# Wider selection, sum and maximum-spread products in the first 24 heads of a batched decode attention block

## The chip, the cores and the metric

The kernel runs on one core of one Trainium2 chip. The metric is the device time of one execution in microseconds (us); lower is better. The engines are named as in the profile: PE is TensorE's matmul stream, PEld its weight loads, DVE is VectorE, ACT is ScalarE, POOL is GpSimd and SP is SyncE, which issues nearly all DMAs here.

## The reference, cut to what matters

An adaLN-conditioned decode step for four batch rows, one token each. It has cached attention (32 query heads that share 8 key/value heads, 4,096 cached positions, head size 128, all in float32), then a token-mixing MLP.

```python
mod = (silu(c) @ w_mod).reshape(4, 6, 1, 512)
h = layernorm(x) * (1 + ca) + sa
q = (h @ wq) ...                              # 32 heads of 128
scores = einsum("bhqd,bhkd->bhqk", q, k) * 128 ** -0.5
o = einsum("bhqk,bhkd->bhqd", softmax(scores), v)
x = x + ga * (o.reshape(4, 1, 4096) @ wo)
h = layernorm(x) * (1 + cb) + sb
u = gelu(einsum("bsd,sf->bdf", layernorm(h), w1) + b1)
x = x + gb * (einsum("bdf,fs->bds", u, w2) + b2).transpose
```

The key and value caches are 4 x 8 x 4096 x 128 floats each, 134 MB in all, and every one of them is read once.

## The kernel before

The work goes head by head, over 32 pairs of a batch row and a key/value head ("head i" below, i from 0 to 31; REP = 4 query heads share each). Keys and values come in tiles of 4 MB that hold the key of head i+2 and the value of head i; a ring of three such tiles is shared with the weights that are loaded first (`load_pair`, L174, issued on SP). A tile is free for the next load when the last product that reads it is done, so SP's queue waits for that.

For one head the steps are these, with the line of the main instruction:

- `scores` (L231): eight products of 512 columns, four 32-row quadrants of the result side by side; `row_max` (L236, DVE) takes the maximum of each row.
- `turn_max` (L240, a transpose on PE), `col_max` (L245, DVE), `spread_max` (L251, a product with the constant -1 that puts the negated maximum on all partitions), `copy_max` (L256, DVE), and `expo` (L261, ACT, the exponential and its row sums).
- `turn` (L267/L271, DVE, transposes the probabilities in 32 x 32 blocks), `sums` (L275, one product that adds the row sums up over the blocks and spreads them) and `scale` (L280, DVE, reciprocal).
- `values` (L291): eight products of 512 columns; `copy_v` (L314, DVE) takes the result out of PSUM.
- `pick` (L328): four products with a 128-column stationary block of the copied result and a selection of four columns as the moving operand; they select and add up the pieces and leave a 128 x 4 result. `copy_o` (L335, DVE) multiplies it by the reciprocals, and `project` (L343) and `add_up` (L359, L361, DVE) multiply by the rows of wo and add up.

Every float32 product shows as two weight loads and two matmuls in the trace. So one pick is eight records, one `sums` or `spread_max` is two.

The first 24 heads run in a Python loop that is a little software pipeline: iteration i does scores of head i+2, pick of i-1, transposes and sums of i+1, values of i. From head 8 on the loop also carries the MLP of the batch row that is done (`Mixer`; `expand` L442 on DVE, gelu L506 on ACT, `consume` L453 on PE). The loop ends with values of head 23; the rest of the work, among it pick of head 23 and everything of heads 24 to 31 that is left, stands in a hand-written order, `PLAN` (L667), and after it the last row's MLP (`finish`). Engines take their instructions in the order of the program.

`pick` can already stream its selection several times: `WIDE` (L24) gives the number of copies of the four columns, 24 for head 27 and 32 for head 28. All copies but the first are left unread (`OT[i] = pt[:, 0]`).

Of the kernel before, what the change touches and what calls it, by code (L numbers as in the profile page):

```python
# [8 lines left out]
F32 = mybir.dt.float32  # L9
# [5 lines left out]
B, D, HQ, HKV, SK, DH, F = 4, 512, 32, 8, 4096, 128, 1792  # L15
REP = HQ // HKV
NF = F // 128
EPS = 1e-5
P = 128
NS = B * HKV  # L20
NSM = 3 * NF + 16 + 1


WIDE = {NS - 5: 24, NS - 4: 32}  # L24
NARROW = NS - 3


# [1 line left out]
def adaln_decode(ctx: ExitStack, tc: tile.TileContext, small, x, wmod, wq, kk, kv, vv, wo, out):  # L29
    nc = tc.nc  # L30
    pad = ctx.enter_context(tc.tile_pool(name="pad", bufs=1))
# [7 lines left out]
    ps_m = ctx.enter_context(tc.tile_pool(name="ps_m", bufs=2, space=PSUM))  # L39
    ps_e = ctx.enter_context(tc.tile_pool(name="ps_e", bufs=1, space=PSUM))  # L40
    ctx.enter_context(tc.manual_schedule())
    mm = nc.tensor.matmul
    dv = nc.vector

    neg1 = pad.tile([1, 96], F32, name="neg1")[:, 0:1]
    sm = cst.tile([P, NSM], F32, name="sm")
    xr = wk.tile([P, D], F32, name="xr", tag="yw", bufs=1)[0:B]
    wm01 = ring.tile([P, 2, 4, D], F32, name="wm01", tag="kv")
# [17 lines left out]
    nc.gpsimd.tensor_scalar(w1n, w1, -1.0, None, op0=OP.mult)  # L66
    ones = cst.tile([P, P], F32, name="ones")
    nc.gpsimd.memset(ones, 1.0)
    nc.gpsimd.memset(neg1, -1.0)
    part = cst.tile([P, 1], F32, name="part")  # L70
    nc.gpsimd.memset(part, -1.0 / D)
    half = cst.tile([P, 1], F32, name="half")
# [11 lines left out]
    eight = g32.rearrange("p (r x) -> p r x", x=8)[:, :, 0]  # L84
# [42 lines left out]
    for k in range(4):  # L127
        n = slice(k * P, (k + 1) * P)
# [95 lines left out]
    S, M, PL, RL = {}, {}, {}, {}  # L224
# [22 lines left out]
        M[i] = mx  # L247

    def spread_max(i):
        pb = ps_m.tile([P, 1], F32, name="pb", tag="m")  # L250
        mm(pb, M[i].rearrange("o c r -> o (c r)"), neg1, start=True, stop=True)  # L251
        M[i] = pb

    def copy_max(i):
        nm = wk.tile([P, 1], F32, name="nm")
# [15 lines left out]
            dv.transpose(p, p)  # L271

    def sums(i):
        pl = ps_m.tile([P, REP], F32, name="pl", tag="m")
        mm(pl, PL[i][1].to_broadcast([P, P]), eight, start=True, stop=True)  # L275
        RL[i] = pl

    def scale(i):
        rl = wk.tile([P, REP], F32, name="rl", bufs=4)
# [38 lines left out]
    def pick(i):  # L318
        po = PV.pop(i)
        n, m = po.shape[-1] // DH, WIDE.get(i, 1)  # L320
        if i in OT:
# [290 lines left out]
    for i in range(2):  # L612
        for step in (scores, row_max, turn_max, col_max, spread_max, copy_max, expo):
            step(i)
    for step in (turn, sums, scale):
        step(0)
    mix = None
    for i in range(NS - HKV):
# [7 lines left out]
        if i:  # L626
            pick(i - 1)
            copy_o(i - 1)
        turn(i + 1)
        sums(i + 1)  # L630
        scale(i + 1)
        if i:
# [3 lines left out]
        col_max(i + 2)  # L636
        values(i, range(4))
        spread_max(i + 2)
        copy_max(i + 2)
        expo(i + 2)  # L640
# [16 lines left out]
        if i == NS - HKV - 2:  # L657
# [17 lines left out]
    g T2 zs za zx zq c c zm zb0 T3 zv zb1 zw0 zn zc  # L675
    """
    TABLE = {"s": scores, "S": row_max, "m": turn_max, "X": col_max, "b": spread_max, "B": copy_max, "e": expo,
             "l": sums, "L": scale, "V": copy_v, "a": pick, "A": copy_o, "P": add_up,
             "LP": load_pair}
    MIX = {"F": mix.fold, "R": mix.residual, "G": mix.gather, "M": mix.modulate, "H": mix.gather, "Q": mix.spread,  # L680
# [3 lines left out]
    for step in PLAN.split():  # L684
        op, k = step.rstrip("0123456789."), step.lstrip("abcdefghijklmnopqrstuvwxyzABCDEFGHIJKLMNOPQRSTUVWXYZ")
        i, q = (int(n) for n in (k + ".0").split(".")[:2]) if k else (0, 0)
# [102 lines left out]
```

## Time and profile before

| | |
|---|---|
| median of three runs | 386.45 us (386.39 to 386.74) |
| span of the profiled execution, first to last instruction | 384.7 us |
| median less span (start and end outside the instructions) | 1.75 us |
| mean granted TensorE clock | 0.883 of full speed |
| PE busy / DVE busy / ACT busy | 78% / 52% / 29% of the span |
| moved by DMA | 157.69 MB, mean 410 GB/s |

Times in the trace count from the first instruction. The page names no time of the profiled execution other than its span, so sums are made against the 384.7 us and carried over to the median with the 1.75 us.

### The profile page before, as it was taken

To read this page: it belongs to the slowest core of one execution; us is meant where nothing else is said; L and a number is where in the kernel's file an instruction comes from. 1 tells how busy PE (TensorE), PEld (TensorE's weight loads), DVE (VectorE), ACT (ScalarE), POOL (GpSimd) and SP (SyncE) were. 2 spreads that over 40 slices of the span, in tenths; PEclk is the share of its full clock that TensorE was granted. 3 is DMA by queue.
4 is the path that set the end of the run, shared out by engine and by line. 5 is a ranking of instruction groups with operands and counts; after the bars stand their busy time and mean duration, and the time that the engine had idled before them with its cause. 6 is when DMAs were issued, how large, how long until landed. Compare 5 with 4: busy or idle time off the path is not lost.

```text
span 384.7 us, 5604 instructions
## 1 busy us (share of the span) xinstructions
PE 298.7 (78%) x2380; PEld 117.2 (30%) x2380; DVE 198.2 (52%) x407; ACT 112.2 (29%) x144; POOL 7.7 (2%) x33
## 2 busy tenths in 40 slices
PE   0856777866966949979877878788888887999984
PEld 0112122311323313334322222342222343333653
DVE  1130251620451424664866545557665567778757
ACT  1001111121110110212567311124575105657276
POOL 1100000000000000000000000000000000000000
PEclk9989555985695685998999998999999999999999
DMA  8999999999999999999999999999999999999930
GB/s 331 433 433 436 411 453 433 409 432 436 423 441 433 434 436 436 434 436 431 429 425 433 428 433 434 429 433 431 429 434 436 434 436 432 424 417 423 418 122 3
DMA packets 7409, 157.69 MB, mean 410 GB/s; under 512 B 964, under 2 KB 1236, under 8 KB 1496
## 3 DMA queue, kind: packets, MB, share of 16 engines
q1 hardware_dynamic: 7376, 157.33, 95.4%
q8 instruction: 18, 0.29, 0.3%
q14 instruction: 7, 0.06, 0.0%
q10 hardware_dynamic: 8, 0.00, 0.0%
HBM read 157.32 MB, written 0.01 MB: 409 GB/s over the span
## 4 chain that ended last, share of the span: by engine, by line
DMA 60%; PE 29%; DVE 7%; ACT 2%; issue 1%; POOL 0%; SPq 0%; POOLq 0%; DVEq 0%
DMA kv<-in_kv 58%; PE s L231 8%; PE pv L291 7%; PE s L122 2%; PE qs L138 2%; DVE m L236 2%; DVE p L267 2%; DMA sm<-in_small 2%; PE pa L343 2%; PE pt L328 2%; ACT uu L562 1%; PE pb L251 1%; PE pve L303 1%; PE pm L240 1%; PE pgx L348 1%
## 5 line engine op out<-in xcount | busy, mean ns | idle before, releaser
L231 PE MATMUL s<-kv,QT 128*32 128x512 f32 x512 | 75.2, 714 | 38.9 <-DMA kv<-in_kv 37.0
L236 DVE TENSOR_REDUCE m<-s 128x1 f32<-128x1024 f32 x32 | 39.2, 1224 | 96.0 <-PE s L231 95.9
L261 ACT ACTIVATE p<-s,nm 128x1024 f32<-128x1024 f32 x32 | 35.7, 1115 | 180.6 <-DVE nm L256 180.5
L291 PE MATMUL pv<-kv,p 128*32 128x512 f32 x464 | 69.8, 670 | 0.7 <-DMA kv<-in_kv 0.7
L231 PEld LDWEIGHTS s<-kv,QT 128*32 128x32 f32 x512 | 15.8, 123 | 84.0 <-DMA kv<-in_kv 52.5
L328 PEld LDWEIGHTS pt<-g,po 128*128 128x128 f32 x236 | 31.1, 205 | 27.2 <-issue 19.9
L343 PE MATMUL pa<-wo,oT 128*32 128x512 f32 x240 | 34.6, 648 | 4.6 <-DVE oT L335 4.4
L328 PE MATMUL pt<-g,po 128*128 128x4 f32 (+2 forms) x236 | 33.9, 267 | 1.5 <-DVE po L314 1.0
L267 DVE STREAM_TRANSPOSE p<-p 128x1024 f32<-128x1024 f32 x25 | 30.9, 1234 | 0.0
L314 DVE COPY po<-pv 128x512 f32<-128x512 f32 x29 | 20.0, 688 | 16.8 <-PE pv L291 16.7
L245 DVE TENSOR_REDUCE mx<-pm 1x128 f32<-1x512 f32 x32 | 21.3, 669 | 1.1 <-PE pm L240 1.1
L442 DVE TENSOR_SCALAR u<-hb,wr,sm 128x512 f32<-128x512 f32 x40 | 19.9, 541 | 1.9 <-POOL wr L437 1.0
L506 ACT ACTIVATE u<-u 128x1024 f32<-128x1024 f32 x20 | 20.4, 1051 | 1.5 <-DVE u L442 1.4
L361 DVE TENSOR_TENSOR acc<-acc,pa 128x512 f32<-128x512 f32 x26 | 17.8, 686 | 4.3 <-PE pa L343 4.2
L261 ACT ACT_TABLE_LOAD x11 | 14.1, 1283 | 20.3 <-DVE nm L256 20.2
L251 PEld LDWEIGHTS pb<-neg,mx 1*128 1x128 f32 x64 | 10.4, 202 | 28.2 <-DVE mx L245 26.5
L122 PE MATMUL s<-wm,sT 128*4 128x512 f32 x16 | 9.1, 732 | 10.6 <-DVE sT L108 10.6
L506 ACT ACT_TABLE_LOAD x13 | 16.7, 1283 | 0.2
L291 PEld LDWEIGHTS pv<-kv,p 128*32 128x32 f32 x464 | 13.4, 146 | 7.2 <-issue 3.1
L240 PE MATMUL pm<-ident,m 128*1 128x128 f32 x32 | 9.3, 289 | 7.4 <-DVE m L236 3.5
L251 PE MATMUL pb<-neg,mx 1*128 1x1 f32 x64 | 13.1, 271 | 2.1 <-DVE mx L245 2.1
L453 PE MATMUL py<-u,sm 128*32 128x512 f32 x80 | 14.4, 616 | 0.0
(158 smaller groups left out, 214.7 us busy)
## 6 DMA issues: line engine op xcount, KB each, us to landing
kv<-in_kv SPq DMA_DIRECT2D x28, 4096.0 KB, 21.9
wq<-in_wq SPq DMA_DIRECT2D x2, 4096.0 KB, 16.3
wo<-in_wo SPq DMA_DIRECT2D x4, 2048.0 KB
kv<-in_kv SPq DMA_DIRECT2D x4, 2048.0 KB, 20.3
wm<-in_wmod SPq DMA_DIRECT2D x2, 2048.0 KB, 14.8
kv<-in_kk SPq DMA_DIRECT2D x1, 4096.0 KB
kv<-in_vv SPq DMA_DIRECT2D x3, 1024.0 KB
wm<-in_wmod SPq DMA_DIRECT2D x1, 1024.0 KB
```

The costliest lines, as they stand in the source:

```text
L231: mm(s[32 * c:32 * c + 32, n * 512:(n + 1) * 512], QT[:, b, h, :], KT[i][:, (n * 4 + c) * 512:(n * 4 + c + 1) * 512], start=True, stop=True)
L236: dv.tensor_reduce(M[i], S[i], axis=AX.X, op=OP.max)
L245: dv.tensor_reduce(mx, M[i].rearrange("o (c r) -> o r c", c=4).unsqueeze(1).to_broadcast([1, 4, 32, 4]), axis=AX.X, op=OP.max)
L251: mm(pb, M[i].rearrange("o c r -> o (c r)"), neg1, start=True, stop=True)
L261: nc.scalar.activation(p, S[i], AF.Exp, bias=M.pop(i), accum_out=l)
L267: dv.transpose(PL[i][0], PL[i][0])
L291: mm(PV[i][32 * q:32 * q + 32, :], pT[:, 128 * k:128 * k + 128:4], VT[i][:, 4 * k:4 * k + 4, :].rearrange("p j d -> p (j d)"), start=(k < ...
L314: dv.tensor_copy(PV[i], pv)
L328: mm(pt, po[:, c * DH:(c + 1) * DH], sel.unsqueeze(1).to_broadcast([P, m, REP]), start=(c == 0), stop=(c == n - 1))
L343: mm(pa[32 * g:32 * g + 32, :], oT[:, g:g + 1].to_broadcast([P, 32]), wo_t[h][:, g, :], start=True, stop=True)
L442: dv.tensor_scalar(u[:, e, :], hb, wr[:, j:j + 1], b1[:, j:j + 1], op0=OP.mult, op1=OP.add)
L506: nc.scalar.activation(u, u, AF.Gelu_apprx_tanh)
```

## The change

In heads 0 to 23 three small products stream more columns than are read. `pick` streams its selection of four columns 64 times over (256 columns in place of 4), `sums` streams its four columns 64 times (256 in place of 4), and `spread_max` multiplies by 96 constants in place of one. The readers take the first copy. The tile `neg1` was already 96 wide; its memset on POOL now fills all of it. Number and order of instructions, tiles and buffers stay the same, as do heads 24 to 31.

```diff
-WIDE = {NS - 5: 24, NS - 4: 32}
+WIDE = {NS - 5: 24, NS - 4: 32, **{i: 64 for i in range(NS - HKV)}}
...
-    neg1 = pad.tile([1, 96], F32, name="neg1")[:, 0:1]
+    negs = pad.tile([1, 96], F32, name="neg1")
+    neg1 = negs[:, 0:1]
...
-    nc.gpsimd.memset(neg1, -1.0)
+    nc.gpsimd.memset(negs, -1.0)
...
     def spread_max(i):
-        pb = ps_m.tile([P, 1], F32, name="pb", tag="m")
-        mm(pb, M[i].rearrange("o c r -> o (c r)"), neg1, start=True, stop=True)
-        M[i] = pb
+        n = 96 if i < NS - HKV else 1
+        pb = ps_m.tile([P, n], F32, name="pb", tag="m")
+        mm(pb, M[i].rearrange("o c r -> o (c r)"), negs[:, 0:n], start=True, stop=True)
+        M[i] = pb[:, 0:1]
...
     def sums(i):
-        pl = ps_m.tile([P, REP], F32, name="pl", tag="m")
-        mm(pl, PL[i][1].to_broadcast([P, P]), eight, start=True, stop=True)
-        RL[i] = pl
+        m = 64 if i < NS - HKV else 1
+        pl = ps_m.tile([P, m, REP], F32, name="pl", tag="m")
+        mm(pl, PL[i][1].to_broadcast([P, P]), eight.unsqueeze(1).to_broadcast([P, m, REP]), start=True, stop=True)
+        RL[i] = pl[:, 0]
```

## Rows read from the trace of the kernel before

**Rows 1.** The page: span, PE's busy time, and two lines by 40 slices.
```profile
span 384.7 us, 5604 instructions
PE 298.7 (78%) x2380; PEld 117.2 (30%) x2380; DVE 198.2 (52%) x407; ACT 112.2 (29%) x144; POOL 7.7 (2%) x33
...
PEclk9989555985695685998999998999999999999999
DMA  8999999999999999999999999999999999999930
```
**Rows 2.** The page, DMA issues: KB each, median us from issue to landing.
```profile
kv<-in_kv SPq DMA_DIRECT2D x28, 4096.0 KB, 21.9
```
**Rows 3.** Windows: length, busy us per engine, PEclk, DMA share, GB/s.
```profile
61.50:317.00 255.50, 203.65 (x1463) 76.85 (x1464) 132.41 (x252) 66.70 (x84) 3.20 (x7) 0.88 1.00 432
317.00:369.50 52.50, 48.37 (x567) 24.66 (x569) 39.71 (x94) 28.45 (x32) 0.76 (x2) 0.97 0.98 414
```
**Rows 4.** The page: the chain that ended last, by engine.
```profile
DMA 60%; PE 29%; DVE 7%; ACT 2%; issue 1%; POOL 0%; SPq 0%; POOLq 0%; DVEq 0%
```
**Rows 5.** Timeline of PE, one head: start, length, instruction, [idle before <-releaser].
```profile
191.55 1.92 PE L231 MATMUL s<-kv,QT 128*32 128x512 f32 x16 [1.26 <-DMA kv<-in_kv]
...
193.40 1.05 PE L328 MATMUL pt<-g,po 128*128 128x4 f32 x8
...
201.31 1.92 PE L231 MATMUL s<-kv,QT 128*32 128x512 f32 x16 [1.70 <-DMA kv<-in_kv]
```
**Rows 6.** Groups of PE, 184 to 230 us: busy us, mean ns of one.
```profile
L231 PE MATMUL s<-kv,QT 128*32 128x512 f32 x68 | 8.3, 598 | 5.1 <-DMA kv<-in_kv 5.1
...
L328 PE MATMUL pt<-g,po 128*128 128x4 f32 x40 | 5.3, 255 | 0.0
```
**Rows 7.** Timeline of PE: the pick of head 28, already wider.
```profile
356.11 1.16 PE L328 MATMUL pt<-g,po 128*128 128x128 f32 x8
```
**Rows 8.** A stretch at half clock: its window (columns as rows 3) and its pick.
```profile
120.00:128.00 8.00, 8.00 (x39) 2.90 (x31) 3.88 (x6) 0.00 (x0) 0.00 (x0) 0.50 0.97 418
```
```profile
122.43 1.87 PE L328 MATMUL pt<-g,po 128*128 128x4 f32 x8
```
**Rows 9.** The chain in order of time: start, us, what.
```profile
143.25 3.64 PE s L231 x16
...
155.27 16.91 DMA kv<-in_kv
```
**Rows 10.** Timeline of the last loop heads and the plan's first steps.
```profile
289.74 1.92 PE L231 MATMUL s<-kv,QT 128*32 128x512 f32 x16 [1.62 <-DMA kv<-in_kv]
...
293.08 1.06 PE L343 MATMUL pa<-wo,oT 128*32 128x512 f32 x8 [0.21 <-DVE oT L335]
...
300.07 1.92 PE L231 MATMUL s<-kv,QT 128*32 128x512 f32 x16
...
308.09 1.06 PE L328 MATMUL pt<-g,po 128*128 128x4 f32 x8 [0.81 <-DVE po L314]
...
309.35 1.09 PE L291 MATMUL pv<-kv,p 128*32 128x512 f32 x8 [0.20 <-DMA kv<-in_kv]
```
**Rows 11.** Timeline further on in the plan.
```profile
319.02 1.00 DVE L442 TENSOR_SCALAR u<-hb,wr,sm 128x512 f32<-128x512 f32 x2 [1.02 <-POOL wr L437]
...
325.26 1.93 PE L291 MATMUL pv<-kv,p 128*32 128x512 f32 x8
...
343.17 1.92 PE L231 MATMUL s<-kv,QT 128*32 128x512 f32 x16 [0.60 <-DMA kv<-in_kv]
```
**Rows 12.** Windows around the half-clock stretch in the plan (columns as rows 3).
```profile
322.00:325.40 3.40, 1.99 (x18) 0.89 (x14) 3.40 (x7) 0.36 (x1) 0.00 (x0) 1.00 0.96 414
325.40:328.80 3.40, 3.40 (x13) 0.46 (x11) 1.70 (x5) 3.37 (x4) 0.00 (x0) 0.50 0.98 424
```
**Rows 13.** Timeline: the last two waits for cached values.
```profile
362.58 0.81 PEld L303 LDWEIGHTS pve<-kv,p 128*32 128x32 f32 x32 [0.86 <-DMA kv<-in_vv]
...
367.23 0.14 PEld L303 LDWEIGHTS pve<-kv,p 128*32 128x32 f32 x4 [0.17 <-DMA kv<-in_vv]
```

## The prediction

> **What bounds the kernel now.** I read the page's slices first. PE is busy for 78% of the span, which would make it the suspect, but the two lines under it decide: the 16 DMA engines are at 8 or 9 tenths and more in every slice, until they stop in the 39th, at about 368 us [rows 1]. The windows say it more sharply: from 61.5 to 317 us the DMA share is 1.00 at 432 GB/s, and it is 0.98 from there to 369.5 [rows 3]. No time is left over in the stream. The chain that ended last is DMA for 60%, PE for 29% [rows 4]; the PE pieces in the loop lead from a landing to the issue of a later load, as from 143.25 to 155.27 us [rows 9]. So the end is the end of the stream plus the tail behind it (367.4 to 384.7 us), as long as two things hold: no load is issued so late that the stream runs dry, and PE reaches the last landings on time.
>
> How much room does the first have? A load of 4,096 KB lands 21.9 us after its issue [rows 2]; at 432 GB/s it takes 9.7 us itself, so 12.2 us of earlier loads stand ahead of it. That is how late its issue could be. The smallest such case that I saw on the chain is a landing after 16.91 us [rows 9], which leaves 7.2 us.
>
> And the second? In the loop PE waits for keys: 1.26 and 1.70 us ahead of two scores in a row, 9.76 us apart [rows 5]. In the written-out plan it waits 0.60 us at 343.17, and 0.86 and 0.17 us for two of the last pieces of values [rows 11, 13]. The work behind the last of these runs off PE, DVE and ACT and is not touched by the change.
>
> **The change part by part.** It adds no instruction and no DMA and moves none; it makes records longer. The memset of 96 values in place of one is on POOL, ahead of anything that reads it; I cost it at nothing, since POOL is busy for 7.7 us of the whole span with 33 instructions [rows 1], and this one of them can't grow by more than a fraction of that.
>
> A pass of 256 columns is not in the trace. The scores are the nearest by shape: 16 records in 1.92 us, four quadrants side by side, the last record 0.598 us long, so a step of (1.92 - 0.598) / 3 = 0.44 us for 512 columns, 0.22 for 256 [rows 5, 6]. A narrow pick has eight records in 1.05 us, one of them 0.255, so (1.05 - 0.255) / 7 = 0.114 us each [rows 5, 6]: I take the weight loads of 128 columns to set that pace. Going to 0.22 adds 8 x 0.106 = **0.85 us to a pick** and 2 x 0.106 = **0.21 us to `sums`**. The other bound is drawn from a pick that is wide already: 1.16 us for 128 columns [rows 7], 0.11 over the narrow one; by that slope 256 columns come to 1.27, 0.22 over it, and a quarter of that (0.06) for `sums`. Nothing at all is excluded by the 0.11. I take the upper values: 128 columns are where streaming (0.11 by the scores' step) just meets the weight load's 0.114, so the flat slope ends there. `spread_max` with 96 columns stays under the weight load, and two records at the 128-column pick's 0.11 over eight are 0.03 us. So **a head gains 0.3 to 1.1 us of PE work, 1.1 taken**. At half clock (a narrow pick is 1.87 us there, [rows 8]) the columns cost twice that, some 2.1 us.
>
> A rule speaks differently from the row: the Trainium skill, "TensorE: Matmul & The Clock Gate", section "Back-to-back issue gap". It gives N / 2.4 + 2.5 ns for a lone matmul at full clock: 109 ns for 256 columns, less than the 0.114 us that a record of the narrow pick takes now. By that the pick would gain nothing and the lateness worked out below would be gone; the page's figures are for a 16-bit product, and no record here shows 512 columns at that pace.
>
> Where does the 1.1 us go? In heads 0 to 21 it lies beside the stream: PE's waits of 1.26 and 1.70 us per head [rows 5] take it, and if a heavy head did not have them the 7.2 us of queued loads [rows 9] would. Without that cover each head would cost 1.1 us.
>
> The last heads are different, because the plan behind them is dense. Iteration 22 starts on its landing (1.62 us of wait, enough for the 1.1 carried in) [rows 10]. In it the pick and `sums` are wide: 1.06 us, less the 0.21 that PE waits ahead of the projection [rows 10], 0.85. Iteration 23 starts without a wait at 300.07 [rows 10]; its `sums` and `spread_max` belong to heads 24 and 25 and stay narrow, so 0.85 - 0.21 = 0.64. Pick of head 23 stands in the plan at 308.09: 0.85. Together 2.34, less the 0.20 us of wait at 309.35 [rows 10]: the plan starts **2.1 us late** (0.1 by the low bound). What is late next is the first expand on DVE at 319.02, which waited for POOL and no DMA [rows 11], so nothing is taken off there. Then 0.60 us go at 343.17, 0.86 at 362.58, 0.17 at 367.23 [rows 11, 13]: 2.14 - 1.63 = **0.5 us** at the end, 0 by the low bound. Loads stay out of it: those issued in the plan have landings well behind them, as the 12.2 us above say.
>
> One thing works the other way. From 325.4 to 328.8 us the granted clock is 0.50, the lower of the two levels (1.2 and 2.4 GHz), after 3.4 us in which PE was busy for 2.0 at the upper one [rows 12]. Values of head 25 take 1.93 us in it, as against 1.09 for such a step at full clock [rows 10, 11], 0.84 lost; over the whole stretch half its length, 1.7 us, is the most. If the late plan meets it otherwise and the clock stays up, that pays for what is left of the lateness.
>
> So the sum is 384.7 plus 0 to 0.5 of span, and the median 1.75 above: 386.45 to 386.95. I take 386.6.
>
> **Rivals.** A. *The tail takes the lateness up, no change* (forecast), 386.45 to 386.95. This holds whether the clock rises in the loop's half-clock stretches or not: a faster PE there only waits longer for keys. So "the change doesn't do what it says", the clock staying at half in those stretches, is a rival in the mechanism and the same in time, 386.5; half the chance of A is that.
>
> B. *Slower: the plan can't take it.* The waits of 0.60 and 0.86 us belong to PE; if the late chain in the plan is DVE's (row maxima, expands), they give nothing back, and the 2.1 us arrive at the end, perhaps with the half-clock stretch repeated later (1.7 more). For it: DVE is at work for 39.7 of 52.5 us from 317 on and ACT for 28.5 [rows 3]. Against: PE itself is at 48.4 of 52.5 there, and the key that it waits for at 343 us is DMA's. It decides from 0.8 us of unabsorbed lateness on; price 0.8 to 2.1, so 387.3 to 388.6.
>
> C. *Faster: the clock.* 0.88 of full speed in the loop [rows 3] is a loss that wider products might give back, and if the chain were PE's the fall at 325 us alone is 1.7 us: 384.8. Against it stand the landings at 343 and 362 us, which no PE can advance: the gain is held there to what is behind, nothing. Also, PE is busy for all 8 us of a half-clock window at 120 us [rows 8], so being busy was not enough there. The Trainium skill, the same page, section "HAM oscillation — how this bites in real kernels", has the rule behind this rival: gaps in PE's work throttle its clock, and a kernel should keep it fed. The trace agrees in that the fall at 325.4 us follows 3.4 us of which PE stood idle for 1.4 [rows 12].
>
> D. *Slower: the stream runs dry.* If the clock stays at half in the early heads, a head takes the 12.0 us from its key to the next load's issue [rows 9] and 2.1 more, 14.1 against 9.7 of stream; a slack of 7.2 us is gone in the second such head, and each further one costs 4.4 us: 390 and more. Against it: after the first 70 us no two slices in a row stand at 5 [rows 1].
>
> **How the numbers follow.** About 0.2% (0.8 us) is what a measurement of this kernel can tell from no change. A 0.78, B 0.14, C 0.05, D 0.03. The likeliest is A at 386.6, its own range 386.1 to 387.2: the two ends of the sum, with the 0.3 us by which the three runs differ on either side. The range for eight in ten reaches into B's low end: 385.9 to 387.6. Within 0.2%: A, 0.78. Slower: B and D, 0.17. Faster: C, 0.05.
>
> **What the profile afterwards would show.** Right: 432 GB/s and a DMA share of 1.00 in the loop as now; pick records with 256 columns, a group of eight in about 1.9 us at full clock (1.3 would be the low bound); PE's waits ahead of scores in the loop down by about 1 us a head; values of head 24 begun at about 311 us and not 309.35; waits at 343 and 362 us smaller or gone, the last piece of values used at 367 to 368 us. The granted clock is higher in the slices that stand at 5 and 6 now, with no effect on landings. Wrong: a slice in the loop under 420 GB/s with DMA idle; scores of head 30 later than 344.5 us; or a last product of values later than 368.3 us.

## The result and the profile after

The changed kernel takes 387.55 us at the median of nine executions (386.62 to 388.01), the kernel before 386.45 (386.39 to 386.74, nine). The ratio is 1.002, with a 95% interval of 1.001 to 1.0029: slower by about what can be told from no change, and inside the range. What the median hides is a split. Four executions are at 386.62 to 386.85, five at 387.55 to 388.01, and nothing between. The spans (first to last instruction) split a little differently: five lie at 384.7 to 385.1 and four at 385.7 to 386.0. The execution at 387.55, which is the median itself, has a span of only 384.9; its extra 0.8 us or so lies outside the instructions (2.65 us there, against 1.75 to 2.11 in the other eight). Below, the lower and the upper group are those by span. The traced execution is a lower one: 386.62 us, span 384.8. In the experiments 15 of 64 executions of the kernel before stood at 387.8 to 391.3 us, which pulls the ratios there down and widens their intervals; medians and groups are compared beside them.

The page of the changed kernel, the lines that answer to [rows 1, 2, 4]:

```profile
span 384.8 us, 5618 instructions
...
PE 319.2 (83%) x2380; PEld 129.0 (34%) x2380; DVE 200.6 (52%) x407; ACT 112.2 (29%) x144; POOL 8.0 (2%) x33
...
PEclk9989568998796988999999999999999999999999
DMA  8999999999999999999999999999999999999920
...
DMA 43%; PE 41%; DVE 9%; ACT 3%; issue 1%; POOL 1%; SPq 0%; POOLq 0%; DVEq 0%; ACTq 0%
...
kv<-in_kv SPq DMA_DIRECT2D x28, 4096.0 KB, 20.8
```

PE is busy for 20.5 us more. The granted clock is better in seven of the eight slices that stood at 5 and 6. A load lands 20.8 us after its issue at the median, in place of 21.9; with the stream as fast as before that means an issue some 1.1 us later, at the cost of the queued loads alone. PE's share of the chain went from 29% to 41%, and still the span moved by 0.1 us. The windows say why; they answer to [rows 3]:

```profile
61.50:317.00 255.50, 223.85 (x1443) 88.17 (x1447) 132.65 (x246) 66.70 (x84) 2.80 (x6) 0.95 1.00 432
317.00:369.50 52.50, 48.96 (x581) 25.35 (x576) 41.84 (x100) 28.45 (x32) 1.31 (x3) 1.00 0.97 411
```

The loop's clock rose from 0.88 to 0.95 and the stream is at 432 GB/s and a share of 1.00, as before. A better clock bought no landing.

What a wide product costs stands in the groups of PE from 184 to 230 us, beside [rows 6]:

```profile
L331 PE MATMUL pt<-g,po 128*128 128x256 f32 x40 | 10.0, 392 | 0.0
L232 PE MATMUL s<-kv,QT 128*32 128x512 f32 x64 | 7.7, 597 | 0.7 <-DMA kv<-in_kv 0.6
...
L278 PE MATMUL pl<-g,l 128*128 128x256 f32 x10 | 5.1, 600 | 0.0
...
L253 PE MATMUL pb<-neg,mx 1*128 1x96 f32 x10 | 2.3, 308 | 0.9 <-DVE mx L246 0.9
```

The waits for keys ahead of the scores fell from 5.1 to 0.6 us in this stretch: the wider products took most of PE's free time there.

And the last heads of the loop with the plan's start, in the timeline of PE, beside [rows 10, 11, 13]:

```profile
289.56 1.92 PE L232 MATMUL s<-kv,QT 128*32 128x512 f32 x16 [0.24 <-DMA kv<-in_kv]
291.41 2.00 PE L331 MATMUL pt<-g,po 128*128 128x256 f32 x8
293.25 1.02 PE L278 MATMUL pl<-g,l 128*128 128x256 f32 x2
294.21 1.06 PE L346 MATMUL pa<-wo,oT 128*32 128x512 f32 x8
...
301.20 1.92 PE L232 MATMUL s<-kv,QT 128*32 128x512 f32 x16
...
309.99 2.00 PE L331 MATMUL pt<-g,po 128*128 128x256 f32 x8 [0.81 <-DVE po L317]
311.92 1.09 PE L294 MATMUL pv<-kv,p 128*32 128x512 f32 x8
...
321.01 1.09 PE L294 MATMUL pv<-kv,p 128*32 128x512 f32 x8
...
327.47 1.09 PE L294 MATMUL pv<-kv,p 128*32 128x512 f32 x8
...
343.72 1.92 PE L232 MATMUL s<-kv,QT 128*32 128x512 f32 x16
...
365.92 1.92 PE L306 MATMUL pve<-kv,p 128*32 128x128 f32 x60
```

Further lines of the kernel before, for comparison:

```profile
291.59 1.05 PE L328 MATMUL pt<-g,po 128*128 128x4 f32 x8
292.51 0.36 PE L275 MATMUL pl<-g,l 128*128 128x4 f32 x2
...
319.02 1.10 PE L291 MATMUL pv<-kv,p 128*32 128x512 f32 x8 [0.52 <-DMA kv<-in_kv]
...
361.59 1.04 PE L343 MATMUL pa<-wo,oT 128*32 128x512 f32 x8
...
365.61 2.03 PE L303 MATMUL pve<-kv,p 128*32 128x128 f32 x60
```

Values of head 24 begin at 311.92 in place of 309.35: the plan starts 2.57 us late. Scores of head 30 are 0.55 us late at 343.72 and no longer wait for their key, and the last big group of value products is 0.31 us late at 365.92. The tail behind it ends 0.1 us late. Between 311.92 and 343.72 two microseconds came back, at three places. The first half of values of head 25 waited 0.52 us for cached values at 319.02 before; now it begins at 321.01 and waits for none, 1.99 us late and no longer 2.57. The second half takes 1.09 us at 327.47, where it took 1.93 at half clock before [rows 11]: 0.84. And the 0.60 us of wait for the key of head 30 is gone [rows 11].

### The profile page after: what moved, and what is told of

It is laid out like the page before. It is cut to its first block, busy times and chain, and to the rows that moved or that the text cites. A ratio compares the mean times of both kernels' runs of the same rounds, so it can differ in the third digit from the quotient of the medians.

```text
span 384.8 us, 5618 instructions
## 1 busy us (share of the span) xinstructions
PE 319.2 (83%) x2380; PEld 129.0 (34%) x2380; DVE 200.6 (52%) x407; ACT 112.2 (29%) x144; POOL 8.0 (2%) x33
## 4 chain that ended last, share of the span: by engine, by line
DMA 43%; PE 41%; DVE 9%; ACT 3%; issue 1%; POOL 1%; SPq 0%; POOLq 0%; DVEq 0%; ACTq 0%
DMA kv<-in_kv 41%; PE s L232 8%; PE pt L331 8%; PE pv L294 5%; PE pa L346 4%; PE pl L278 3%; PE s L123 2%; PE qs L139 2%; DVE mx L246 2%; DMA sm<-in_small 2%; DVE acc L364 2%; PE pb L253 2%; PE py L456 1%; ACT uu L565 1%; PE pve L306 1%
## 5 line engine op out<-in xcount | busy, mean ns | idle before, releaser
L232 PE MATMUL s<-kv,QT 128*32 128x512 f32 x512 | 72.5, 690 | 23.4 <-DMA kv<-in_kv 21.3
L294 PE MATMUL pv<-kv,p 128*32 128x512 f32 x464 | 63.9, 617 | 0.0
L331 PE MATMUL pt<-g,po 128*128 128x256 f32 (+3 forms) x236 | 56.6, 380 | 1.3 <-DVE po L317 0.8
L331 PEld LDWEIGHTS pt<-g,po 128*128 128x128 f32 x236 | 41.7, 198 | 30.7 <-issue 15.6
L346 PE MATMUL pa<-wo,oT 128*32 128x512 f32 x240 | 31.8, 602 | 0.5 <-DVE oT L338 0.3
L278 PE MATMUL pl<-g,l 128*128 128x256 f32 (+1 forms) x64 | 27.8, 518 | 0.2 <-ACT p L263 0.2
L253 PE MATMUL pb<-neg,mx 1*128 1x96 f32 (+1 forms) x64 | 14.5, 305 | 6.3 <-DVE mx L246 6.1
L338 DVE TENSOR_TENSOR oT<-pt,rl 128x4 f32<-128x4 f32 x30 | 4.8, 161 | 21.0 <-PE pt L331 20.9
## 6 DMA issues: line engine op xcount, KB each, us to landing
kv<-in_kv SPq DMA_DIRECT2D x28, 4096.0 KB, 20.8
```

The costliest lines, as they stand in the source:

```text
L232: mm(s[32 * c:32 * c + 32, n * 512:(n + 1) * 512], QT[:, b, h, :], KT[i][:, (n * 4 + c) * 512:(n * 4 + c + 1) * 512], start=True, stop=True)
L253: mm(pb, M[i].rearrange("o c r -> o (c r)"), negs[:, 0:n], start=True, stop=True)
L278: mm(pl, PL[i][1].to_broadcast([P, P]), eight.unsqueeze(1).to_broadcast([P, m, REP]), start=True, stop=True)
L294: mm(PV[i][32 * q:32 * q + 32, :], pT[:, 128 * k:128 * k + 128:4], VT[i][:, 4 * k:4 * k + 4, :].rearrange("p j d -> p (j d)"), start=(k < ...
L331: mm(pt, po[:, c * DH:(c + 1) * DH], sel.unsqueeze(1).to_broadcast([P, m, REP]), start=(c == 0), stop=(c == n - 1))
L346: mm(pa[32 * g:32 * g + 32, :], oT[:, g:g + 1].to_broadcast([P, 32]), wo_t[h][:, g, :], start=True, stop=True)
```

## The experiments

Theory L (late plan) holds the last heads of the loop responsible, theory E (everywhere) all 24 heads. For the first four kernels the kernel before had a median of 386.51 us on the same chip (35 executions).

**The changed kernel again**, with no edit:

> The changed kernel once more, unedited, as the measure for the other three and for a second trace. Theory L (late plan: the wide products of the last heads of the loop make the written-out plan start 2.6 us late, and an execution ends near 386.8 or near 387.6 depending on whether the clock then falls in the plan): 386.6 to 388.0 again in two groups, and a trace of the upper group shows a half-clock stretch between 320 and 370 us. Theory E (the wide products of all heads cost a little each): all executions near 387.3, one group, and nothing in the plan differs.

Median 386.93 us of twelve executions, 386.46 to 387.74, ratio 0.9985 (0.9958 to 1.0013). Seven lie up to 387.02 and five from 387.27 on, less cleanly parted than the first time. The trace is of a lower one (386.55) and has the clock at full through the plan. Theory E's single group near 387.3 did not come. The trace of an upper execution came later, with the single executions below.

**Wide in heads 0 to 20 only:**

```diff
-WIDE = {NS - 5: 24, NS - 4: 32, **{i: 64 for i in range(NS - HKV)}}
+WIDE = {NS - 5: 24, NS - 4: 32, **{i: 64 for i in range(21)}}
...
-        n = 96 if i < NS - HKV else 1
+        n = 96 if i < 21 else 1
...
-        m = 64 if i < NS - HKV else 1
+        m = 64 if i < 21 else 1
```

> Wide only for heads 0 to 20, so the plan starts on its landing at 309.35 us again. Theory L: 386.45 as before, all executions within 0.3 us of it. Theory E: 21 of 24 parts of what the full change costs, about 387.3. Rival clock theory (more PE work earlier changes the clock in the plan wherever it stands): two groups as in the full change.

Median 386.57 us; eleven of twelve at 386.42 to 386.71, one at 391.26; ratio 0.9988 (0.9955 to 1.002). That is the kernel before. In its trace the windows and the plan's start are:

```profile
61.50:317.00 255.50, 221.31 (x1461) 87.33 (x1462) 134.47 (x252) 66.70 (x84) 3.20 (x7) 0.95 1.00 432
```
```profile
309.50 1.09 PE L294 MATMUL pv<-kv,p 128*32 128x512 f32 x8 [0.45 <-DMA kv<-in_kv]
...
325.44 1.94 PE L294 MATMUL pv<-kv,p 128*32 128x512 f32 x8
...
343.34 1.92 PE L232 MATMUL s<-kv,QT 128*32 128x512 f32 x16 [0.62 <-DMA kv<-in_kv]
```

Nearly all of the extra work and of the clock gain is in it (221.31 us of PE, against 203.65 before and 223.85 in the full change; clock 0.95), and the plan starts on its landing. Theory E falls. The half-clock stretch at 325 us is here, and with the plan on time it costs nothing.

**Wide in heads 21 to 23 only:**

```diff
-WIDE = {NS - 5: 24, NS - 4: 32, **{i: 64 for i in range(NS - HKV)}}
+WIDE = {NS - 5: 24, NS - 4: 32, **{i: 64 for i in range(21, NS - HKV)}}
...
-        n = 96 if i < NS - HKV else 1
+        n = 96 if 21 <= i < NS - HKV else 1
...
-        m = 64 if i < NS - HKV else 1
+        m = 64 if 21 <= i < NS - HKV else 1
```

> Wide only for heads 21, 22 and 23. Theory L: the same as the full change, 386.6 to 388.0 with a median near 387.4, and values of head 24 at about 311.9 us. Theory E: 3 of 24 parts, 386.6 at most, one group.

Median 387.45 us, ratio 0.9991 (0.9964 to 1.0019). Five executions are at 386.76 to 386.91, seven at 387.41 to 387.77: the two groups of the full change from an eighth of its heads. The traced execution is of the upper group, 387.49 us, span 385.7:

```profile
311.97 1.09 PE L294 MATMUL pv<-kv,p 128*32 128x512 f32 x8
...
327.70 1.94 PE L294 MATMUL pv<-kv,p 128*32 128x512 f32 x8
...
344.60 1.92 PE L232 MATMUL s<-kv,QT 128*32 128x512 f32 x16
```

The start is that of the full change; at 327.70 the values run at half clock (1.94 us), and scores of head 30 and the end are 0.9 us later than in the lower group's trace.

**All 24 heads, 128 columns** in pick and sums:

```diff
-WIDE = {NS - 5: 24, NS - 4: 32, **{i: 64 for i in range(NS - HKV)}}
+WIDE = {NS - 5: 24, NS - 4: 32, **{i: 32 for i in range(NS - HKV)}}
...
-        m = 64 if i < NS - HKV else 1
+        m = 32 if i < NS - HKV else 1
```

> All 24 heads wide, but 128 columns in pick and sums in place of 256 (spread of the maximum as in the change). A pick of 128 columns took 1.16 us before against 1.05 for four columns, so 0.1 us a pick and 0.03 a sum: values of head 24 at 309.4 to 309.7 us. Theory L: 386.45 to 386.6, one group. Theory E, if it goes by the count of wide products and not by columns: 387.3; if by time, 386.6 as well.

Median 386.62 us, ratio 0.9983 (0.9956 to 1.001). Ten executions are at 386.41 to 386.80, two at 387.48 and 387.88. These two are not an upper group: their spans are 384.7 and 384.9, as in the other ten (384.5 to 384.7), and the extra time lies outside the instructions. The traced one (386.55) starts the plan at 309.12, not late at all. Its pick and `sums` in iteration 22:

```profile
291.49 1.16 PE L331 MATMUL pt<-g,po 128*128 128x128 f32 x8
292.49 0.60 PE L278 MATMUL pl<-g,l 128*128 128x128 f32 x2
```

The pick costs 0.11 us more than the narrow one. `sums` costs 0.24 more (0.60 in place of 0.36), against 0.03 expected; nearly all of it falls into the 0.21 us that PE waited ahead of the projection before [rows 10]. The number of wide products is that of the full change and the time is that of the kernel before, so it is the time which the products take that counts, not their number.

For the second four kernels the kernel before had a median of 386.53 us (29 executions, another chip).

**Two picks of 512 columns**, heads 22 and 23:

```diff
-WIDE = {NS - 5: 24, NS - 4: 32, **{i: 64 for i in range(NS - HKV)}}
+WIDE = {NS - 5: 24, NS - 4: 32, 22: 128, 23: 128}
...
-        n = 96 if i < NS - HKV else 1
+        n = 1
...
-        m = 64 if i < NS - HKV else 1
+        m = 1
```

> Only the picks of heads 22 and 23 are wide, with 512 columns each; sums and spreads as before. A 256-column pick holds PE for 1.84 us in the changed kernel against 0.92 narrow, so one of 512 columns takes about 3.7, 2.75 more; two of them less the 0.20 us of wait: the plan starts 5.3 us late. Theory L: after the waits of 0.60, 0.86 and 0.17 us, 3.7 us are left at the end, or 2.0 if a half-clock stretch in the plan falls away: 388.4 to 390.2. Rival F (the lateness itself is free and only a fall of the clock in the plan costs, once): 387.6 at most.

Median 389.09 us of ten, ratio 1.0055 (1.0029 to 1.0081). Six are at 388.85 to 389.14, four at 389.59 to 390.03. In the trace (389.04 us, span 387.2) the two picks and the start of the plan:

```profile
302.07 3.71 PE L331 MATMUL pt<-g,po 128*128 128x512 f32 x8
...
310.72 3.71 PE L331 MATMUL pt<-g,po 128*128 128x512 f32 x8 [0.82 <-DVE po L317]
314.36 1.10 PE L294 MATMUL pv<-kv,p 128*32 128x512 f32 x8
...
329.91 1.09 PE L294 MATMUL pv<-kv,p 128*32 128x512 f32 x8
...
346.16 1.93 PE L232 MATMUL s<-kv,QT 128*32 128x512 f32 x16
```

The plan is 5.0 us late at the start, 3.0 at scores of head 30 and 2.5 at the end, with the clock at full (329.91). Rival F, one fixed price, falls: against the lower trace of the full change the plan starts 2.44 us later (314.36 and 311.92) and the span is 2.4 us longer (387.2 and 384.8). What is late beyond the waits of the plan arrives whole.

**Heads 0 to 20 with 512-column picks**, the cover of the loop taken away:

```diff
-WIDE = {NS - 5: 24, NS - 4: 32, **{i: 64 for i in range(NS - HKV)}}
+WIDE = {NS - 5: 24, NS - 4: 32, **{i: 128 for i in range(21)}}
...
-        n = 96 if i < NS - HKV else 1
+        n = 96 if i < 21 else 1
...
-        m = 64 if i < NS - HKV else 1
+        m = 64 if i < 21 else 1
```

> As the kernel with heads 0 to 20 wide, but their picks stream 512 columns: 2.75 us more than narrow, with sums and spread 3.2 a head. Theory L says that the 1.3 us of the change were hidden in heads 0 to 20 because PE waited 1.3 to 1.7 us a head for keys, and 7 to 12 us of loads were queued. With 3.2 that cover is gone from head 8 on, where the MLP runs too: 13 heads late by 1.5 to 1.9 us each, 20 to 25 us in all, of which the queue and the narrow heads behind take about 12: 395 to 400, and a DMA share clearly under 1.00 in the loop. If the loop's work were hidden for another reason (PE not in the way at all), 386.5.

Median 399.1 us of two, ratio 1.0304 (1.0233 to 1.0375). From 200 to 317 us, this kernel first, then the full change:

```profile
200.00:317.00 117.00, 113.03 (x682) 39.93 (x680) 65.67 (x123) 43.38 (x50) 1.31 (x3) 1.00 0.96 393
```
```profile
200.00:317.00 117.00, 107.49 (x731) 43.23 (x727) 70.08 (x133) 42.73 (x50) 1.30 (x3) 1.00 1.01 433
```

PE is busy for 113.03 of the 117 us, the loads come late, and the stream falls to 393 GB/s. So the waits for keys and the queued loads were what hid the change in the loop, and the change used most of the waits.

**Only the pick of head 23:**

```diff
-WIDE = {NS - 5: 24, NS - 4: 32, **{i: 64 for i in range(NS - HKV)}}
+WIDE = {NS - 5: 24, NS - 4: 32, 23: 64}
...
-        n = 96 if i < NS - HKV else 1
+        n = 1
...
-        m = 64 if i < NS - HKV else 1
+        m = 1
```

> Only the pick of head 23 is wide, with 256 columns: the plan starts 0.7 to 0.9 us late. Theory L: the waits of 0.60 and 0.86 us take all of it, 386.45 to 386.6, one group. If a late plan costs whatever its size, 387.2 to 387.5.

Median 386.44 us, all ten at 386.35 to 386.63, ratio 0.9983 (0.9958 to 1.0009). The plan starts at 309.92 in place of 309.35, the second half of values of head 25 meets a half-clock stretch, and scores of head 30 still wait 0.49 us for their key:

```profile
309.92 1.09 PE L294 MATMUL pv<-kv,p 128*32 128x512 f32 x8
...
319.00 1.09 PE L294 MATMUL pv<-kv,p 128*32 128x512 f32 x8
...
325.46 1.43 PE L294 MATMUL pv<-kv,p 128*32 128x512 f32 x8
...
343.07 1.92 PE L232 MATMUL s<-kv,QT 128*32 128x512 f32 x16 [0.49 <-DMA kv<-in_kv]
```

A small lateness is swallowed whole, also with the clock down. What swallowed it is not the waits of 0.60 and 0.86 us that were expected to: at 319.00 PE is already on time again (319.02 before), so the 0.57 us went into the wait of 0.52 for cached values there.

**The full change with wide spreads up to head 27**, an attempt to keep the clock up:

```diff
-        n = 96 if i < NS - HKV else 1
+        n = 96 if i < NS - 4 else 1
```

> The full change, and the spread of the maximum streams 96 columns up to head 27 in place of head 23, so that PE does a little more in the stretch of the plan after which the clock falls in some executions (it waits for DVE from 324.9 to 327.5 us). If the upper group comes from that fall and the fall from PE's little work there: one group, 386.6 to 386.9. If the spreads change nothing of that: two groups as in the full change, 386.5 to 387.8.

Median 387.92 us of twelve (386.65 to 389.39), ratio 1.0006 (0.9973 to 1.0039). Two are below 387, one at 387.15, nine at 387.73 and above. The attempt failed: the upper group did not go, it holds more of the executions. The trace was of the lowest one (386.65, span 384.9), clock at full through the plan.

Last, four single executions with traces, to see both groups of one kernel (386.44 us before).

> The changed kernel, one more trace, to tie the group of an execution to the clock in its plan. Theory L: an execution at 386.5 to 386.9 shows the clock at full from 310 us to the end of the plan and scores of head 30 at 343.6 to 343.9 us; one at 387.3 to 387.8 shows a half-clock stretch between 321 and 345 us, scores of head 30 about 0.9 us later, and no wait for cached values behind. Rival: an upper execution with the clock at full throughout and the extra 0.9 us elsewhere (landings later, or the tail behind 369 us longer).

> As the run before it: the changed kernel, one more trace, same expectations of both theories.

The first is a lower execution (386.80 us, span 385.0), the second an upper one (387.44, span 385.7). The windows of the plan, lower first:

```profile
322.00:326.00 4.00, 3.09 (x29) 0.73 (x21) 4.00 (x9) 1.94 (x2) 0.00 (x0) 1.00 0.96 410
326.00:330.00 4.00, 3.21 (x19) 1.41 (x19) 2.30 (x7) 2.50 (x4) 0.00 (x0) 1.00 1.01 434
330.00:334.00 4.00, 3.54 (x32) 1.15 (x34) 4.00 (x8) 3.97 (x4) 0.00 (x0) 1.00 1.08 467
334.00:369.50 35.50, 34.12 (x452) 18.86 (x450) 28.12 (x71) 18.94 (x23) 0.00 (x0) 1.00 0.95 401
```
```profile
322.00:326.00 4.00, 2.90 (x30) 0.67 (x22) 4.00 (x10) 1.71 (x2) 0.00 (x0) 1.00 0.92 395
326.00:330.00 4.00, 3.47 (x15) 1.21 (x17) 2.30 (x6) 2.73 (x4) 0.00 (x0) 0.68 0.99 426
330.00:334.00 4.00, 4.00 (x34) 1.26 (x34) 2.51 (x6) 3.97 (x4) 0.00 (x0) 0.89 1.12 483
334.00:369.50 35.50, 34.12 (x443) 18.55 (x436) 29.00 (x71) 18.20 (x22) 0.00 (x0) 1.00 0.95 402
```

The same kernel, nearly the same start of the plan (312.13 and 311.91 us), the same 34.12 us of PE work behind 334: what differs is the clock from 326 to 334. Scores of head 30 in the lower one, and three steps of the upper one:

```profile
343.93 1.92 PE L232 MATMUL s<-kv,QT 128*32 128x512 f32 x16
```
```profile
321.00 1.09 PE L294 MATMUL pv<-kv,p 128*32 128x512 f32 x8
...
344.57 1.92 PE L232 MATMUL s<-kv,QT 128*32 128x512 f32 x16
...
366.76 1.92 PE L306 MATMUL pve<-kv,p 128*32 128x128 f32 x60
```

The scores are 0.64 us apart, 0.86 when counted from the start of the plan; that is the price of the half-clock step (1.94 us in place of 1.09). The spans are 0.7 apart, so nothing is added behind 344 us, and neither of the two scores waits for its key. The rival, landings or the tail, is out.

> The kernel with spreads of 96 columns up to head 27, one more trace. Ten of its twelve executions were at 387.1 to 389.4 us, the traced one at 386.7. Theory L: an upper execution shows a half-clock stretch in the plan, as for the changed kernel. Rival: the wider spreads of heads 24 to 27 lengthen the plan's own chain by about 1 us with the clock at full.

387.79 us, span 386.0, an upper execution: half clock again, 0.80 from 326 to 330 and 0.77 from 330 to 334. The wider spreads do not lengthen the plan by themselves: the lower execution of this kernel has a span of 384.9, the full change 384.8 to 385.0.

> The kernel with heads 21 to 23 wide, one more trace. Its traced execution was of the upper group (387.5 us) with a half-clock stretch at 327 us. Theory L: an execution at 386.8 has the clock at full there or the stretch elsewhere, and the same start of the plan at 311.9 to 312.0 us. Rival: the start of the plan differs between the groups.

386.70 us, span 384.9, a lower one: plan from 312.04, clock 1.00 throughout, scores of head 30 at 343.83. So for the full change and for heads 21 to 23 alone each group is traced, and each time the half-clock stretch goes with the upper one.

## Why the prediction was right, and where it was off

**The bound.** Right, and shown: the stream ran at 432 GB/s with either kernel, the work in heads 0 to 20 cost nothing (386.57 us), and it cost 12.6 us when the cover was gone (399.1). Rival C (faster by the clock) is refuted with it: the loop's clock rose to 0.95, and the key that iteration 22 waits for came at 289.56 in place of 289.74, no more than 0.2 us earlier. Rival D did not come; the loop's clock is up, not down.

**The price of a column.** The pick was sized well: the upper bound gave 0.22 us a record, and (2.00 - 0.392) / 7 = 0.23 is what the trace has; a pick holds PE for 1.84 us in place of 0.92 (0.92 more; 0.85 said). A pick of 512 columns takes 3.71 us against 2.00, so it goes nearly by columns there. The Trainium skill's 109 ns ("TensorE: Matmul & The Clock Gate", "Back-to-back issue gap") does not hold for these float32 records; 0.23 us was measured. **`sums` was mis-sized:** 0.21 us said. Two records of 256 columns take 1.02 us, one of them 0.600, so 0.42 a record, nearly twice the pick's. From its start to the projection it held PE for 0.96 us in place of 0.36. It filled the 0.21 us of wait that I had counted as cover, and cost iteration 22 another 0.39 us. A head thus gained 1.5 us from these two products at full clock, more than the 1.1 that I gave as the most for a head.

**The lateness of the plan.** 2.1 us said, 2.57 measured: iteration 22 took 11.64 us from scores to scores in place of 10.33 (1.31 more, 0.85 said), iteration 23 0.77 more to the pick of head 23 (0.64 said), that pick 0.67 beyond the landing (0.65 said). The sum of 2.75 starts 0.18 earlier.

**What is left at the end.** The time is near the sum, but the path to it is not the one that I wrote, and part of the agreement is luck. I took off waits of 0.60, 0.86 and 0.17 us, 1.63 in all; 2.57 - 1.63 = 0.94, and the upper group's span of 385.7 is 1.0 over the 384.7 of before. The traces divide it otherwise. At 319 us I looked at the wait of DVE for POOL and took nothing off; PE waited there as well, 0.52 us for cached values, and in the upper trace the step begins at 321.00, 1.98 us late in place of 2.56. At scores of head 30 it is 1.40 late, so the 0.60 was rightly counted. From there to the last big group of values (366.76) only 0.25 us more goes, though the 0.86 lies in between. That is a wait of the weight loads, PEld; PE itself was at work on a projection from 361.59 to 362.63 and could give back little. A wait that I left out and one that I counted in full nearly cancel.

The rest of the error is the lateness, 0.4 us more than said, most of it by the `sums` term. In the lower group the half-clock stretch fell away and paid for most of what is left (spans 0.1 to 0.3 us over the one before). I named that stretch as something that would pay, but put one number between the two; the two outcomes lie side by side. By span four of nine and five of twelve executions of the full change (one of them at 385.3, between the two groups) and seven of twelve with heads 21 to 23 wide lie in the upper group. By the marks set before, the lower group passes (scores of head 30 at 343.62 to 343.93 us) and the upper fails (344.57 and 344.60, past the 344.5). That the median of 387.55 lies inside the range, 0.05 us from its end, is luck too: it is the time of one execution with a lower span and 2.65 us outside its instructions, and three of the nine lie beyond 387.6.

Rival B said that DVE would hold the waits back and that they would give nothing. That is not what the upper group is: the lateness there falls at PE's waits for cached data, from 2.56 us to 1.40 by scores of head 30. Its time of 387.3 and up was met by another way, a lateness larger than the waits.

**What stays open.** Why one execution meets the stretch and the next, of the same program, does not. PE was busy for 2.90 of the 4 us from 322 on ahead of a fall, and for 2.90 and 3.09 without one in two other traces of the same kernel; with wider spreads it was busy for 3.21 ahead of a fall. So its busy share there does not part them. Why the kernel with wider spreads falls more often was not settled either, nor what the executions with 2.65 to 2.98 us outside their instructions spend it on. None of the long executions of the kernel before was traced. Their spans (386.1 us and up) are longer than those of the upper executions of the full change (385.3 to 386.0), but whether they have a cause in common is not shown.

None of the kernels beats the one before; 386.44 us with one wide pick is the same time. The stream sets it.

## What to carry to other kernels

Padding a small product to keep PE's clock up costs little as long as its records stay near the pace of their weight loads, and its full streaming time above that; measure it for each product. Here 128 columns added 0.11 us to the pick but 0.24 to `sums`, 256 columns 0.92 and 0.60. In a stage that waits for a saturated stream, neither the cost nor the better clock shows; what shows is what the padding leaves behind at the seam to the next stage, so stop it some heads earlier (here at head 20) where that stage is dense. When a lateness is set against waits further on, go through every wait of the late engine itself; a wait of its weight loads may cover work that it still has to do. When a median lies between two groups, compare spans and trace an execution of each before explaining it.

## What the runs showed of the hardware that was not expected

A record of 256 columns took 0.23 us in the pick and 0.42 in `sums`, both with a 128-column stationary operand and the same 256 results. The moving columns differ: every second float of a row in the pick, every eighth in `sums`. And the stationary operand of `sums` is one column read 128 times. The runs with 128 and 256 columns have the same stationary operands, and from one to the other a record of `sums` grows by 1.6 ns a column ((1.02 - 0.60) / 2 / 128), one of the pick by 0.8 ((2.00 - 1.16) / 8 / 128). So the extra time of `sums` goes with the number of moving columns, but no run here changes one of the two operands alone.

The same program on the same chip met a half-clock stretch of PE at 326 us in some executions and not in others, with the plan begun at the same time to 0.2 us. In the kernel before the stretch is free: PE meets it and still waits 0.60 us for its key at 343 us [rows 11, 12].
